# Loading the first x tile in two column pieces, one on each DMA queue, with 15 warm-up matmuls instead of 18

## The chip, the cores and the metric

The kernel runs on one core of a Trainium2 chip. The metric is the device time of one execution in microseconds (us). The profile's span, from the first to the last instruction, is about 1.8 us shorter than that time.

## The reference

A two-layer network with SiLU, forward and backward, all in bf16:

```python
# x [1, 2048, 640], w1 [640, 1536], w2 [1536, 640], grad_out like x
h = jnp.einsum("bsd,df->bsf", x, w1)
out = jnp.einsum("bsf,fd->bsd", silu(h), w2)
# returned: out, and the gradients of x, w1 and w2 for grad_out
```

## The kernel before

The change touches only the first microseconds. The core starts its loads before anything else, and TensorE runs matmuls on a constant tile ("warm-ups") until x arrives. Three tiles of 128 rows of x (x0, x1, x2) are transposed on TensorE; then the product h = x·w1 starts with row block 0 of w1, whose columns 0 to 511 and 512 to 1023 are loaded separately. SyncE (SP) and ScalarE (ACT) each feed one DMA queue (q1 and q10 of the page: 146960 and 288 packets in before).

```python
    NWARM = 18
    ...
        early = [nc.vector.memset(warm[:], 1.0)]
        ...
        for i in range(NWARM):
            early.append(nc.tensor.matmul(wp[:, 0:P], lhsT=warm[:], rhs=warm[:], start=True, stop=True))
    ...
        def load_x(eng, q):
            return eng.dma_start(out=x_nat[:, q, :], in_=x_v[:, q, :])
    ...
        early += [load_x(nc.sync, 0), load_x(nc.scalar, 1), load_x(nc.sync, 2)]
        early += [load_w1(0, slice(0, FC), nc.scalar), load_w1(0, slice(FC, FA))]
        early += [load_w1(k, slice(0, FA)) for k in range(1, 3)]
        ...                                   # row blocks 3 and 4, the rest of w1
        nc.sync.dma_start(out=w2_nat[:], in_=w2_v[:])
        goT_next = load_goT(0)
    ...
        def pe_x(xT):                         # 5 transposes for each of x0, x1, x2
            ...
        def h_first(xT, aT, ghT):
            pe_x(xT)
            ...
            for dt_ in range(DT):             # row blocks of w1
                for ft in range(NA):          # ft 0..3 read columns 0..511, ft 4..7 the others
                    mm(ft, dt_, slice(0, HC), dt_ == 0, False)      # 384 columns of xT (x0, x1, x2)
            ...                               # then the last 128 columns, then 512-column matmuls
```

Of the kernel before, what the change touches and what calls it, by code (L numbers as in the profile page):

```python
# [75 lines left out]
def kernel(  # L76
# [11 lines left out]
    nc = tc.nc  # L88
    P = 128
# [6 lines left out]
    S, D = x2.shape  # L96
# [6 lines left out]
    NFC = F // FC  # L103
    FB = FC // P
    LAG = 2
    NWARM = 18
    NQ = 3
    HC = NQ * P
    NA = 8
    FA = NA * P  # L110
# [15 lines left out]
    x_nat = natpool.tile([P, ST, D], dt_in, name="x_nat")  # L126
# [3 lines left out]
    x_v = x2.rearrange("(st p) d -> p st d", p=P)  # L130
# [17 lines left out]
    with ExitStack() as mctx:  # L148
# [9 lines left out]
        early = [nc.vector.memset(warm[:], 1.0)]  # L158
        warm_a = cpool.tile([P, 1], FP32, name="warm_a")
        wp = ps_h.tile([P, SC], FP32, name="wp", tag="hp")  # L160
        for i in range(NWARM):
            early.append(nc.tensor.matmul(wp[:, 0:P], lhsT=warm[:], rhs=warm[:], start=True, stop=True))
# [18 lines left out]

        xT_next = xpool.tile([P, DT, SC], dt_in, name="xT")

        def load_x(eng, q):
            return eng.dma_start(out=x_nat[:, q, :], in_=x_v[:, q, :])

        def load_w1(k, cols=slice(0, F), eng=nc.sync):
            return eng.dma_start(out=w1_nat[:, k, cols], in_=w1_v[:, k, cols])

        early += [load_x(nc.sync, 0), load_x(nc.scalar, 1), load_x(nc.sync, 2)]  # L190
        early += [load_w1(0, slice(0, FC), nc.scalar), load_w1(0, slice(FC, FA))]
        early += [load_w1(k, slice(0, FA)) for k in range(1, 3)]
        for k in range(3, DT):
            load_w1(k, slice(0, FA))
        nc.sync.dma_start_transpose(out=xT_next[:, :, HC:SC], in_=x2[HC:SC, :])
        nc.sync.dma_start(out=w1_nat[:, :, FA:F], in_=w1_v[:, :, FA:F])
# [34 lines left out]
        def silu_a(ft, hp, aT):  # L231
            nc.scalar.activation(aT[:, ft, :], hp[:], ACT.Silu)  # L232
# [16 lines left out]
        def h_first(xT, aT, ghT):  # L249
# [3 lines left out]
            def mm(ft, dt_, cols, start, stop):  # L253
                nc.tensor.matmul(  # L254
                    hs[ft][:, cols],
                    lhsT=w1_nat[:, dt_, ft * P:(ft + 1) * P],
                    rhs=xT[:, dt_, cols],
                    start=start,
                    stop=stop,
                )  # L260

            for dt_ in range(DT):
                for ft in range(NA):
                    mm(ft, dt_, slice(0, HC), dt_ == 0, False)
            for ft in range(NA):
                for dt_ in range(DT):
                    mm(ft, dt_, slice(HC, SC), False, dt_ == DT - 1)
                silu_a(ft, hs[ft], aT)
# [48 lines left out]
        for c in range(NCH):  # L317
# [10 lines left out]
            if c == 2:  # L328
                for j in range(0, ST, STC):
                    rows = slice(max(j, NQ), j + STC)  # L330
                    nc.sync.dma_start(out=x_nat[:, rows, :], in_=x_v[:, rows, :])

            if c == 0:
                h_first(xT, aT, ghT)
                nc.sync.dma_start(
                    out=aT_scr[:, c * SC:(c + 1) * SC].rearrange("(ft p) s -> p ft s", p=P), in_=aT[:]
                )
                sd_phase(c, w2_nat, aT, oT_scr)
                for ft in range(FT):
                    g_group(ft, goT, ghT)  # L340
                nc.sync.dma_start(
                    out=ghT_scr[:, c * SC:(c + 1) * SC].rearrange("(ft p) s -> p ft s", p=P), in_=ghT[:]
# [4 lines left out]
            for i in range(FT + LAG):  # L347
# [7 lines left out]
                out=aT_scr[:, c * SC:(c + 1) * SC].rearrange("(ft p) s -> p ft s", p=P), in_=aT[:]  # L355
            )
            nc.sync.dma_start(
                out=ghT_scr[:, c * SC:(c + 1) * SC].rearrange("(ft p) s -> p ft s", p=P), in_=ghT[:]
# [7 lines left out]
    with ExitStack() as fctx:  # L366
# [45 lines left out]
        for fc in range(NFC):  # L412
            gh_blk = gh_blks[fc]
            for dt_ in range(DT):
                if dt_ == DT // 2:
                    store_gw2(fc)
                if fc == NFC - 1 and dt_ == DT - 1:
                    last_stores = []
                    for k, (lo, hi) in enumerate(((0, FC - P), (FC - P, FC))):
# [12 lines left out]
                        else:  # L432
                            nc.vector.tensor_copy(out=g1[:, lo:hi], in_=gp[:, lo:hi])  # L433
                        store = nc.sync.dma_start(
                            out=gw1_v[:, dt_, fc * FC + lo:fc * FC + hi], in_=g1[:, lo:hi]
# [50 lines left out]
```

## Time and profile before

| | before |
|---|---|
| time, median of the first 3 runs | 319.7 us (319.48 to 320.14) |
| span of the profiled run | 318.5 us |
| TensorE (PE) busy | 315.5 us |
| first transpose, first h matmul | 2.85 us, 4.53 us |
| first 512-column matmul of h | 13.86 us |

The page of the profile first: busy time with its share of the span, then the chain that ended last.

```profile
span 318.5 us, 3634 instructions
...
PE 315.5 (99%) x1529; PEld 147.5 (46%) x1529; DVE 103.0 (32%) x183; ACT 77.4 (24%) x139; POOL 0.7 (0%) x6
...
PE 98%; DMA 1%; DVE 0%; issue 0%; DVEq 0%; SPq 0%
```

TensorE is the bottleneck nearly throughout, so work can be saved only at the start or the end. Now the start of the same chain in order of time. The columns are start, length (both us) and what the time was spent in.

```profile
...
0.08 2.73 DMA x_nat<-in_x_dram
2.81 0.05 issue
2.85 1.78 PE tp L212 x15
4.64 9.39 PE hp L254 x80
14.03 4.32 PE hp L223 x20
18.34 11.87 PE hp L302 x55
```

The chain starts with the load of x0, runs through the 15 transposes, and then stays on TensorE. Next is the timeline of the matmuls (PE) and their weight loads (PEld) of before: start, length, line, tiles, count, and in brackets the idle time before the group and what ended it. Here and below, "..." marks lines left out.

```profile
...
0.51 2.10 PE L162 MATMUL wp<-warm 128*128 128x128 bf16 x18 [0.51 <-DVE warm L158]
2.85 1.78 PE L212 MATMUL tp<-ident,x_nat 128*128 128x128 bf16 x15 [0.24 <-DMA x_nat<-in_x_dram]
...
4.33 0.31 PEld L254 LDWEIGHTS <-w_nat 128*128 128x128 bf16 x2
4.53 9.50 PE L254 MATMUL hp<-xT,w_nat 128*128 128x384 bf16 x80
...
4.80 0.15 PEld L254 LDWEIGHTS <-w_nat 128*128 128x128 bf16 x1 [0.17 <-issue]
...
5.12 0.15 PEld L254 LDWEIGHTS <-w_nat 128*128 128x128 bf16 x1 [0.17 <-issue]
5.45 0.72 PEld L254 LDWEIGHTS <-w_nat 128*128 128x128 bf16 x4 [0.17 <-issue]
...
6.42 7.44 PEld L254 LDWEIGHTS <-w_nat 128*128 128x128 bf16 x72 [0.25 <-DMA w_nat<-in_w_dram]
...
13.86 4.48 PE L223 MATMUL hp<-xT,w_nat 128*128 128x512 bf16 x20
```

The single weight loads at 4.80, 5.12 and 5.45 us are 0.32 us apart: this is a 384-column matmul at half clock. Later ones are 0.16 us apart and merge into one line. The trace's clock record says the same: full speed from 5.71 us. The PE clock row of the page is too coarse to show this. PE idled only 0.45 us before x0, and 0.10 us before the first h matmul. Idle times in this text are counted so: from start to start, less one matmul. The brackets count from a modelled end, and so show less (0.24).

### The profile page before, as it was taken

How to read it: one execution, taken by the hardware profiler on the slowest of the kernel's cores; microseconds unless marked ns; L12 is line 12 of the kernel's file. 1: busy time of each engine (PE TensorE's matmuls, PEld its weight loads, DVE VectorE, ACT ScalarE, POOL GpSimd, SP SyncE). 2: the span in 40 equal slices, each digit the busy share in tenths (PEclk: the TensorE clock that was granted, in tenths of full speed). 3: DMA queues.
4: the chain of work that ended last, by engine and by line, in shares of the span. 5: the costliest groups of instructions: out<-in, count | busy, mean ns of one | idle time of the engine just before them, and what ended most of it. 6: DMA issues, size and time to landing. Idle time of an engine off the chain costs nothing.

```text
span 318.5 us, 3634 instructions
## 1 busy us (share of the span) xinstructions
PE 315.5 (99%) x1529; PEld 147.5 (46%) x1529; DVE 103.0 (32%) x183; ACT 77.4 (24%) x139; POOL 0.7 (0%) x6
## 2 busy tenths in 40 slices
PE   9999999999999999999999999999999999999997
PEld 6644444444444444444444444444444444444444
DVE  1387641477410187710147741000000100001001
ACT  3492000644201354411064520110100001001010
POOL 0000000000000000000000000000000000000000
PEclk9999999999999999999999999999999999999999
DMA  9999999999799874492635079919999999996011
GB/s 242 332 182 190 238 283 239 350 291 311 233 229 320 199 228 113 145 302 83 166 105 145 0 259 268 216 24 299 254 243 261 251 209 341 245 264 217 33 35 49
DMA packets 147264, 66.85 MB, mean 210 GB/s; under 512 B 113328, under 2 KB 146736, under 8 KB 147248
## 3 DMA queue, kind: packets, MB, share of 16 engines
q1 hardware_dynamic: 146960, 66.33, 82.6%
q10 hardware_dynamic: 288, 0.30, 0.3%
q8 instruction: 12, 0.20, 0.2%
q14 instruction: 4, 0.03, 0.0%
HBM read 9.18 MB, written 28.97 MB: 120 GB/s over the span
## 4 chain that ended last, share of the span: by engine, by line
PE 98%; DMA 1%; DVE 0%; issue 0%; DVEq 0%; SPq 0%
PE hp L302 33%; PE hp L286 16%; PE hp L391 16%; PE hp L442 15%; PE hp L223 14%; PE hp L254 3%; PE hp L422 1%; DMA x_nat<-in_x_dram 1%; PE tp L212 1%; DVE g L433 0%; DVEq L433 0%; SPq L470 0%
## 5 line engine op out<-in xcount | busy, mean ns | idle before, releaser
L286 PE MATMUL hp<-goT,w2T 128*128 128x512 bf16 x240 | 56.9, 379 | 0.0
L302 PE MATMUL hp<-aT,w_nat 128*128 128x512 bf16 x240 | 52.5, 379 | 0.0
L302 PE MATMUL hp<-ghT,w1T 128*128 128x512 bf16 x240 | 52.5, 379 | 0.0
L391 PE MATMUL hp<-a_blk,go_nat 128*128 128x512 bf16 x240 | 52.0, 379 | 0.0
L442 PE MATMUL hp<-gh_blk,x_nat 128*128 128x512 bf16 x224 | 48.5, 379 | 0.0
L223 PE MATMUL hp<-xT,w_nat 128*128 128x512 bf16 x200 | 48.2, 379 | 0.0
L310 ACT ACTIVATE oT<-hp 128x512 bf16<-128x512 f32 x24 | 14.4, 598 | 104.3 <-PE hp L302 104.3
L232 ACT ACTIVATE aT<-hp 128x512 bf16<-128x512 f32 x48 | 28.5, 614 | 37.4 <-PE hp L223 30.4
L302 PEld LDWEIGHTS <-w1T 128*128 128x128 bf16 x240 | 23.5, 98 | 28.3
L302 PEld LDWEIGHTS <-w_nat 128*128 128x128 bf16 x240 | 23.5, 98 | 28.3 <-DMA w_nat<-in_w_dram 0.2
L391 PEld LDWEIGHTS <-go_nat 128*128 128x128 bf16 x240 | 23.5, 98 | 28.3
L286 PEld LDWEIGHTS <-w2T 128*128 128x128 bf16 x240 | 23.5, 98 | 28.3
L293 DVE SCALAR_TENSOR_TENSOR ghT<-ghT,hp 128x512 bf16<-128x512 bf16 x48 | 32.5, 682 | 7.0 <-PE hp L286 7.0
L442 PEld LDWEIGHTS <-x_nat 128*128 128x128 bf16 x224 | 21.9, 98 | 26.4
L312 DVE CAST oT<-hp 128x512 bf16<-128x512 f32 x16 | 11.0, 691 | 70.6 <-PE hp L302 70.6
L239 DVE SCALAR_TENSOR_TENSOR ghT<-aT,v 128x512 bf16<-128x512 bf16 x48 | 32.6, 686 | 0.3
L223 PEld LDWEIGHTS <-w_nat 128*128 128x128 bf16 x200 | 19.5, 98 | 23.4
L238 DVE TENSOR_SCALAR v<-t 128x512 bf16<-128x512 f32 x48 | 20.1, 425 | 28.1 <-ACT t L236 28.1
L236 ACT ACTIVATE t<-hp 128x512 f32<-128x512 f32 x44 | 26.5, 620 | 0.0
L453 DVE CAST g<-hp 128x512 bf16<-128x512 f32 x7 | 4.8, 692 | 47.0 <-PE hp L442 28.0
L401 DVE CAST g2T<-hp 128x512 bf16<-128x512 f32 x7 | 4.8, 692 | 46.1 <-PE hp L391 46.1
L399 ACT ACTIVATE g2T<-hp 128x512 bf16<-128x512 f32 x8 | 4.8, 597 | 47.0 <-PE hp L391 47.0
(24 smaller groups left out, 43.7 us busy)
## 6 DMA issues: line engine op xcount, KB each, us to landing
aT_scr<-aT SPq DMA_DIRECT2D x4, 1536.0 KB, 6.2
ghT_scr<-ghT SPq DMA_DIRECT2D x4, 1536.0 KB, 8.0
out_dram<-o_sb SPq DMA_DIRECT2D x8, 640.0 KB, 3.5
oT_scr<-oT SPq DMA_DIRECT2D x4, 640.0 KB, 4.3
go_nat<-in_grad_out_dram SPq DMA_DIRECT2D x4, 640.0 KB, 6.5
gxT_scr<-oT SPq DMA_DIRECT2D x4, 640.0 KB, 5.7
w_nat<-in_w_dram SPq DMA_DIRECT2D x1, 1920.0 KB, 12.5
x_nat<-in_x_dram SPq DMA_DIRECT2D x3, 640.0 KB, 7.0
```

The lines of the kernel that those rows point to most:

```text
L223: nc.tensor.matmul(hp[:], lhsT=w1_nat[:, dt_, ft * P:(ft + 1) * P], rhs=xT[:, dt_, :], start=(dt_ == 0), stop=(dt_ == DT - 1),)
L232: nc.scalar.activation(aT[:, ft, :], hp[:], ACT.Silu)
L236: nc.scalar.activation(t[:], hp[:], ACT.Tanh, scale=0.5)
L238: nc.vector.tensor_scalar(out=v[:], in0=t[:], scalar1=-0.5, scalar2=0.5, op0=ALU.mult, op1=ALU.add)
L239: nc.vector.scalar_tensor_tensor(out=ghT[:, ft, :], in0=aT[:, ft, :], scalar=1.0, in1=v[:], op0=ALU.subtract, op1=ALU.mult)
L286: nc.tensor.matmul(gp[:], lhsT=w2T[:, dt_, ft * P:(ft + 1) * P], rhs=goT[:, dt_, :], start=(dt_ == 0), stop=(dt_ == DT - 1),)
L293: nc.vector.scalar_tensor_tensor(out=ghT[:, ft, :], in0=ghT[:, ft, :], scalar=1.0, in1=gp[:], op0=ALU.add, op1=ALU.mult)
L302: nc.tensor.matmul(op_[:], lhsT=w_all[:, ft, dt_ * P:(dt_ + 1) * P], rhs=rhs_all[:, ft, :], start=(ft == 0), stop=(ft == FT - 1),)
L310: nc.scalar.activation(oT[:, dt_, :], op_[:], ACT.Copy)
L312: nc.vector.tensor_copy(out=oT[:, dt_, :], in_=op_[:])
L391: nc.tensor.matmul(gp[:], lhsT=go_nat[:, st, dt_ * P:(dt_ + 1) * P], rhs=a_blk[:, st, :], start=(st == 0), stop=(st == ST - 1),)
L442: nc.tensor.matmul(gp[:], lhsT=x_nat[:, st, dt_ * P:(dt_ + 1) * P], rhs=gh_blk[:, st, :], start=(st == 0), stop=(st == ST - 1),)
```

## The change

It aims to have x0 on chip sooner: 256 of its 640 columns on SyncE's queue and the other 384 on ScalarE's, ahead of x1 and x2. With x0 sooner, fewer warm-ups fill the wait.

```diff
-    NWARM = 18
+    NWARM = 15
     NQ = 3
+    HD = 2 * P
...
-        def load_x(eng, q):
-            return eng.dma_start(out=x_nat[:, q, :], in_=x_v[:, q, :])
+        def load_x(eng, q, cols=slice(0, D)):
+            return eng.dma_start(out=x_nat[:, q, cols], in_=x_v[:, q, cols])
...
-        early += [load_x(nc.sync, 0), load_x(nc.scalar, 1), load_x(nc.sync, 2)]
+        early += [load_x(nc.sync, 0, slice(0, HD)), load_x(nc.scalar, 0, slice(HD, D))]
+        early += [load_x(nc.sync, 1), load_x(nc.scalar, 2)]
         early += [load_w1(0, slice(0, FC), nc.scalar), load_w1(0, slice(FC, FA))]
```

## The prediction

> **What bounds the kernel now.** TensorE. On the page, PE is busy 315.5 us of a 318.5 us span, and the chain of waits is 98% PE and 1% "DMA x_nat<-in_x_dram": the start, until the first x tile is in. Only that start can change. In the chain in order of time: DMA of x until 2.81 us, 15 transposes of x from 2.85, the matmuls of h from then on without a gap.
>
> **The start, from the trace's single records.** Landings: x0 2.81, x1 3.23, x2 3.63, both pieces of w1 row block 0 by 4.33, w1 block 1 6.37, block 2 7.11 us. Warm-up matmuls come every 107 ns from 0.51 to about 2.40; PE then waits 0.45 us for x0. Transposes come every 107 ns and end near 4.43; x1 and x2 are in before PE needs them. The first h matmul starts at 4.53, after a VectorE copy. Matmuls of 384 columns are 320 ns apart until 5.71 and 163 ns after: the clock record turns to full speed there. PE asks for w1 block 1 at 6.39, which landed at 6.37: no slack. Block 2 has over 0.5 us.
>
> **The DMA side.** On each DMA engine x0, x1 and x2 follow each other: completion packets of x0 and of x1 (other queue) are 420 ns apart, x1 to x2 420 to 480. So x0 does not share its engines with x1; it is already served first. A 1280-byte packet takes 55 ns, 1024 takes 46, 2048 takes 84. By that line (estimate) 512 bytes take 27 and 768 take 37: 8 + 8 packets are 0.51 us, against 0.44 in one piece. What makes x0 late is the start: first packets from 1.12, some stalled for 0.5 to 0.7 us, which splitting does not remove. [...]
>
> **What the change does (estimates).**
> - Columns 0 to 255 of x0 land 0.2 us sooner (2.6), the rest at about 2.9, 0.07 later than all of x0 now. Two transposes start early, three wait.
> - x1 and x2 land 0.07 later (3.30, 3.70). PE then waits for x1: transposes end near 4.37, not 4.43. Gain 0.06 us.
> - w1 block 1 may be 0.07 later (6.44), which eats that gain. Net on the path -0.05 to +0.05 us.
> - ScalarE issues one more DMA (0.4 us), so its table load ends near 2.9; its first copy is at 4.14: free.
> - Three warm-ups fewer: they were off the path. [...]
>
> **Prediction.** 319.6 us, range 319.2 to 320.2. Faster by over 2%: 0.5%; within 2%: 99%; slower: 0.5%. The spread of before (0.66 us) exceeds the effect.
>
> **What would show it.** Right: first transpose near 2.6, a wait for x0's second piece and for x1, first h matmul at 4.4 to 4.55, w1 block 1 asked for at 6.3 to 6.45. Wrong: all of x0 in before 2.6, first h matmul before 4.3[...].

The marked cuts took out a rule on turns of the DMA queues, an allowance for a later full clock in some runs, and the sign that went with it: no trace of this case had shown them. The terms sum to -0.05 to +0.05 us on the path. The forecast was 319.6 us, beside the 319.7 us of before's first runs; the 0.1 us between them lies within their spread (0.66 us).

## The result, and the profile after

| | before | after |
|---|---|---|
| time, median of 6 runs each | 320.19 us (319.48 to 320.91) | 322.35 us (321.67 to 323.21) |
| ratio | | 1.0069 (1.0044 to 1.0093) |
| span of the profiled run | 318.5 us | 321.0 us |
| x0 wholly landed | 2.81 us | 2.33 us |
| x1 landed | 3.23 us | 3.71 us |
| first half of w1 block 0 landed | 4.01 us | 5.42 us |
| first h matmul | 4.53 us | 5.47 us |
| full clock from | 5.71 us | 9.92 us |
| first 512-column matmul of h | 13.86 us | 16.39 us |

The change is within 2%, but clearly slower: about 2.2 us. The page of after:

```profile
span 321.0 us, 3601 instructions
...
PE 315.4 (98%) x1498; PEld 147.6 (46%) x1526; DVE 103.0 (32%) x183; ACT 77.4 (24%) x139; POOL 0.7 (0%) x6
...
PE 98%; DMA 1%; issue 1%; DVE 0%; SPq 0%; DVEq 0%
```

Busy time is as before; the span is 2.5 us longer. (The trace lacks some matmul records: 1498, beside 1526 weight loads.) The start of the chain of after:

```profile
...
0.54 3.17 DMA x_nat<-in_x_dram
3.71 0.05 issue
3.75 1.26 PE tp L214 x10
5.02 0.02 issue
5.04 0.44 DVE xT L219
5.48 11.08 PE hp L256 x80
```

The chain no longer starts with x0. It starts with the load issued at 0.54 us, x1, and only 10 transposes are on it; the 80 matmuls of h take 11.08 us instead of 9.39. The timeline of after, same columns:

```profile
...
0.51 1.78 PE L163 MATMUL wp<-warm 128*128 128x128 bf16 x15 [0.51 <-DVE warm L159]
2.15 0.73 PE L214 MATMUL tp<-ident,x_nat 128*128 128x128 bf16 x5
...
3.75 1.25 PE L214 MATMUL tp<-ident,x_nat 128*128 128x128 bf16 x10 [0.88 <-DMA x_nat<-in_x_dram]
...
5.46 0.13 PEld L256 LDWEIGHTS <-w_nat 128*128 128x128 bf16 x2 [0.73 <-DMA w_nat<-in_w_dram]
5.47 11.09 PE L256 MATMUL hp<-xT,w_nat 128*128 128x384 bf16 x80 [0.47 <-DVE xT L219]
...
9.28 0.15 PEld L256 LDWEIGHTS <-w_nat 128*128 128x128 bf16 x1 [0.17 <-issue]
9.60 0.15 PEld L256 LDWEIGHTS <-w_nat 128*128 128x128 bf16 x1 [0.17 <-issue]
9.92 6.46 PEld L256 LDWEIGHTS <-w_nat 128*128 128x128 bf16 x65 [0.17 <-issue]
...
16.39 3.83 PE L225 MATMUL hp<-xT,w_nat 128*128 128x512 bf16 x16
```

There are two waits: for x1 (1.08 us between the fifth transpose and the sixth) and for the first half of w1 block 0 (0.67 us). The chain names a VectorE copy for the second one, since that copy ended at 5.47; but the weight load's own line names the DMA of w, which landed at 5.42. In before the first h matmul started 0.57 us ahead of the end of the same copy, so the copy is not what it needs. After that, weight loads stay 0.32 us apart until 9.92 us: 14 matmuls at half clock, against 4.

The two parts add up. The first h matmul is 0.94 us later, and 10 more matmuls cost 0.157 us more each (320 less 163 ns): 0.94 + 1.57 = 2.51 us. The 512-column matmuls start 2.53 us later, the span is 2.5 us longer, and nothing is lost after that.

### The profile page after: what moved, and what is told of

It is laid out like the page before. It is cut to its first block, busy times and chain, and to the rows that moved or that the text cites. A ratio compares the mean times of both kernels' runs of the same rounds, so it can differ in the third digit from the quotient of the medians.

```text
span 321.0 us, 3601 instructions
## 1 busy us (share of the span) xinstructions
PE 315.4 (98%) x1498; PEld 147.6 (46%) x1526; DVE 103.0 (32%) x183; ACT 77.4 (24%) x139; POOL 0.7 (0%) x6
## 4 chain that ended last, share of the span: by engine, by line
PE 98%; DMA 1%; issue 1%; DVE 0%; SPq 0%; DVEq 0%
PE hp L304 32%; PE hp L288 16%; PE hp L393 16%; PE hp L444 15%; PE hp L225 13%; PE hp L256 3%; PE hp L424 1%; DMA x_nat<-in_x_dram 1%; PE tp L214 0%; DVE xT L219 0%; SPq L186 0%; DVE g L435 0%; DVEq L435 0%; SPq L472 0%
```

## The experiments

The theories. **Clock theory**: TensorE idles too much in the early microseconds, so full clock comes later, and the slow matmuls are the loss. **Arrival theory**: data come later, PE waits for them, and the clock follows along or matters little. Both can hold in part; the runs were to split the 2.2 us. All runs gave correct results, each in 5 rounds against before on the same chip; ratios are to before. "Lands" and "full clock" are from the one profiled run of each kernel. The landing times of all of them stand in one table after the last experiment.

### k1_warm15: only fewer warm-ups

```diff
-    NWARM = 18
+    NWARM = 15
```

> Before with 15 warm-up matmuls, loads untouched. Clock theory (the time is lost because [...] full clock comes later): PE idles about 0.75 us before the first transpose instead of 0.45, so full clock comes somewhat later on average; +0.1 to +0.7 us, ratio 1.0005 to 1.002. Arrival theory (the time is lost because the split makes x1 and the first w1 pieces land late, and PE waits for them): loads as before, so 0, ratio 1.000 within 0.0007; the first h matmul near 4.53 us.

Measured: 320.34 us, ratio 1.0009 (0.9992 to 1.0026). No difference is shown; a cost of the size that the clock theory named is not excluded. The warm-ups alone are not the loss.

### k2_split18: only the split

The changed kernel with `NWARM = 18`.

> The split loads with 18 warm-up matmuls. Both theories: most of the loss is here. Clock theory: the gaps for x1 and for w1 block 0 remain, the gap before the first transpose is about nil; ratio 1.004 to 1.007, full clock after 7 us in the profile. Arrival theory: first h matmul near 5.4 us and ratio about 1.007, as with 15. If instead the number of warm-ups were the cause: ratio 1.000.

Measured: 322.27 us (319.67 to 323.11), ratio 1.0052 (1.0022 to 1.0083). The loads carry most of the loss. This kernel's profiled run was one of its quick ones (320.78 us): w1 block 0 was as late as in after (5.56 us), but the clock was already full when the first h matmul came at 5.61, and the 512-column matmuls started at 14.36 us. So the expected "full clock after 7 us" failed in this profile. It shows late data without a late clock: 0.5 us behind before, not 2.5.

### k3_split15_fill: the changed kernel with 16 unread matmuls, so that PE has no gaps

```diff
+    FILL = (10, 0, 6)
...
+        def fill(n):
+            for _ in range(n):
+                nc.tensor.matmul(wp[:, 0:P], lhsT=warm[:], rhs=warm[:], start=True, stop=True)
...
+                    fill(FILL[q])             # in the source after the transposes of tile q; on the chip before all of them
```

> The changed kernel plus 16 matmuls on the constant tile that nobody reads: 10 after the transposes of x0 and 6 after those of x2, where PE idled 1.1 and 0.7 us. They bring no data earlier. Clock theory: full clock comes by 7 us; the time falls by 1.2 to 2 us against the changed kernel, ratio to before 1.001 to 1.003. Arrival theory: no gain, ratio 1.007 or more.

Measured: 320.9 us, ratio 1.0024 (1.0008 to 1.0039). The chain of this kernel's start:

```profile
...
0.51 1.78 PE wp L164 x15
2.29 1.71 PE wp L210 x16
3.99 1.60 PE tp L219 x15
5.59 9.28 PE hp L262 x80
```

The edit did not do what the expectation says. All sixteen unread matmuls (line 210) ran straight after the warm-ups, before the first transpose, which began at 3.79 us instead of 2.15. So they did not fill the gaps. They held the transposes back until x1 was in (3.37 us), and no gap opened: after 0.51 us PE idled only 0.10 us. The first h matmul came at 5.48 us, as in after (5.47), here because the transposes were late, for w1 was in at 4.49. In this profile the loads came sooner than in after, as they vary from run to run, but that gained nothing, since the first h matmul was no earlier. Yet about two thirds of the loss went (ratio 1.0024 instead of 1.0069), with full clock at 6.52 us instead of 9.92. This is the clock theory's run, and it holds.

### k4_warm8: the gap alone, loads untouched

```diff
-    NWARM = 18
+    NWARM = 8
```

> Before with 8 warm-up matmuls: PE idles from 1.36 us to the landing of x0 near 2.8; loads untouched. Clock theory: [...] +0.6 to +1.6 us, ratio 1.002 to 1.005, and more spread. Arrival theory: the warm-ups are off the data path, ratio 1.000 within 0.0007.

Measured: 321.03 us, ratio 1.0029 (1.001 to 1.0047). In the profile the data were even early, and the first h matmul came at 4.26 us; the clock was full at 6.76 only. PE idle time costs 0.9 us here with no change in any load. The arrival theory can't give this.

### k5_split15_fill5: a smaller filling

As k3 with `FILL = (5, 0, 0)`. These five too ran before the first transpose, like five more warm-ups.

> The changed kernel with only 5 unread matmuls after the transposes of x0 and none before the first h matmul: about 0.5 us of PE idle taken away where x1 is waited for, and no delay added. Clock theory [...]: better than the changed kernel by 1 us or more, ratio to before 1.000 to 1.003; full clock by 7 us in most runs. Arrival theory (late x1 and w1 block 0 alone): as the changed kernel, 1.006 to 1.007.

Measured: 320.69 us (319.89 to 322.66), ratio 1.0031 (1.0004 to 1.0058). Four runs had spans of 318.1 to 319.2 us and two had 320.9. Full clock may have come later in those two, since the last gap stayed open; that is a guess, and no profile of them shows it. In the profile full clock came at 3.44 us, w1 block 0 at 5.74.

### k6_warm22: before with more warm-ups

`NWARM = 22` in before.

> Before with 22 warm-up matmuls instead of 18, so that PE idles hardly at all before x0 lands at 2.6 to 2.8 us. Clock theory: [...] ratio 0.9985 to 1.000; first h matmul at most 0.1 us later. Arrival theory: 1.000.

Measured: 320.52 us, ratio 1.0009 (0.9997 to 1.0021). The clock theory's gain did not come. Full clock came at 5.48 us, 0.23 us sooner than in before, but PE then waited 0.40 us for w1 block 1 (in at 6.62). In this profile that wait ate the quicker start. There was no wait for w2, which landed at 18.18 us; its product started at 18.43.

### k7_split15_x2sp: w1 block 0 back to second place on ScalarE's queue

```diff
-        early += [load_x(nc.sync, 1), load_x(nc.scalar, 2)]
+        early += [load_x(nc.sync, 1), load_x(nc.sync, 2)]
```

> The changed kernel with x2 on the SyncE queue, so that the ScalarE queue carries the second piece of x0 and then the first piece of w1 block 0, as the second of its queue as in before. If the late landing of w1 block 0 (5.4 and 5.6 us in two of three profiles of the split) comes from its place as third on ScalarE's queue, that piece lands by 4.5 us and the ratio falls to 1.002 or less. If it comes from slow packets of w1 whatever the place, the ratio stays at 1.004 to 1.007.

Measured: 321.67 us, ratio 1.0046 (1.0031 to 1.0062). The first half of w1 landed at 3.77 us, as expected of its place in the queue. The ratio did not fall as expected: PE still idled 0.78 us for x1, full clock came at 8.49 us, and most of what followed on SyncE's queue came later (w1 block 2, say, at 8.70 us instead of 7.29). Half right.

### k8_whole_swap: the exchange of x1 and x2 without a split

```diff
-        early += [load_x(nc.sync, 0), load_x(nc.scalar, 1), load_x(nc.sync, 2)]
+        early += [load_x(nc.sync, 0), load_x(nc.sync, 1), load_x(nc.scalar, 2)]
```

> Before (18 warm-up matmuls, x0 whole on SyncE), but with x1 on SyncE and x2 on ScalarE, as the change has them. If the exchange of queues is the cost: ratio 1.003 or more. If the split of x0 is: ratio 1.000 within 0.0015, x0 in by 2.8 us, w1 block 0 by 4.5 us.

Measured: 320.8 us, ratio 1.0023 (1.0011 to 1.0035), spans all 319.0 to 319.5. x1 landed at 3.61 us instead of 3.23: the second place on SyncE's queue costs it that with x0 whole too. Full clock came early (4.67 us), and the 512-column matmuls started at 13.52 us, ahead of before. The lead was lost afterwards. The waits of PE in its first 20 us, in total, times, longest:

```profile
PE hp L302 <- DMA w_nat<-in_w_dram: 0.6, 1, 0.6
PE wp L162 <- DVE warm L158: 0.5, 1, 0.5
PE tp L212 <- DMA x_nat<-in_x_dram: 0.4, 1, 0.4
```

The first line is new: PE waits for w2, which landed at 18.58 us here and at 18.04 in before. A quicker start can run into this floor.

### k9_before_w2halves and k10_swap_w2halves: w2 in two halves

```diff
-        nc.sync.dma_start(out=w2_nat[:], in_=w2_v[:])
+        for lo in range(0, FT, FT // 2):
+            nc.sync.dma_start(out=w2_nat[:, lo:lo + FT // 2, :], in_=w2_v[:, lo:lo + FT // 2, :])
```

> Before with w2 loaded in two halves of its 12 row blocks, first half first. In the profiles of before the product with w2 started at 18.18 us and w2 had landed at 18.04: a floor just under the start. If that floor counts: runs whose full clock comes early gain up to 0.5 us, ratio 0.9980 to 0.9995. If it does not: 1.000 within 0.0007.

Measured: 319.55 us (319.38 to 319.87) against 320.31, ratio 0.9977 (0.9965 to 0.9989). This beats both kernels, by 0.7 us. In its profile the first half of w2 landed at 13.26 us, the second at 17.36, and PE went on at 17.76 without a wait. The gain is measured; that the floor is all of it is only argued, since in this one profile even the second half was in time.

> The kernel with x1 and x2 exchanged between the queues (x0 whole, 18 warm-ups; ratio 1.0023) with w2 in halves. In its profile PE was ahead of before (512-column matmuls from 13.52 us, before 13.86) and then waited 0.6 us for w2, in at 18.58. If that wait was its whole loss: ratio 0.9985 to 1.0005, and no wait for w2 in the profile. If not: 1.002 stays.

Measured: 320.64 us (319.66 to 322.35), ratio 1.0019 (0.9996 to 1.0042). The wait for w2 is gone from the profile (PE went on at 18.25 us, the second half was in at 16.08), but the mean did not move clearly from the 1.0023 of k8, and spans now spread from 317.9 to 320.6 us. Inconclusive on how much of k8's loss the floor was.

### k11_rowhalves: x0 split by rows instead of columns

```diff
-        early += [load_x(nc.sync, 0, slice(0, HD)), load_x(nc.scalar, 0, slice(HD, D))]
+        early += [
+            eng.dma_start(out=x_nat[h:h + 64, 0, :], in_=x_v[h:h + 64, 0, :])
+            for eng, h in ((nc.sync, 0), (nc.scalar, 64))
+        ]
```

> The changed kernel (15 warm-ups, three loads on ScalarE's queue), but x0 split by partitions: 64 rows of 1280 bytes on each queue, as many descriptors as before. If the short reads of 512 and 768 bytes make the first w1 pieces late: they land by 4.6 us and the ratio is 1.001 to 1.003. If the place as third on ScalarE's queue or the earlier order does: they land after 5 us and the ratio is 1.005 to 1.007.

Measured: 323.07 us, ratio 1.0083 (1.0053 to 1.0113); the first half of w1 landed at 5.85 us, full clock came at 8.60. The loss stays without short reads. (Here the second load of each queue was also issued later, at 0.72 us and 0.79 instead of 0.54 and 0.62.)

### k12_split15_w1one: w1 block 0 as one load

```diff
-        early += [load_w1(0, slice(0, FC), nc.scalar), load_w1(0, slice(FC, FA))]
+        early += [load_w1(0, slice(0, FA))]
```

> The changed kernel, but w1 block 0 as one load of 1024 columns on SyncE instead of two of 512 on two queues: as many loads and descriptors before the matmuls as before, two loads on ScalarE's queue. If the extra load (descriptors, third on the queue) makes w1 block 0 late: it lands by 4.6 us, ratio 1.001 to 1.004. If the short reads of x0 do: after 5 us, ratio 1.005 to 1.008.

Measured: 321.54 us, ratio 1.0045 (1.0031 to 1.0058); w1 block 0 landed at 5.14 us, 15 of its 16 shares by 4.67. Between the two expectations; inconclusive on its own.

### k13_whole_w1third: no split, w1 block 0 in third place

```diff
-        early += [load_x(nc.sync, 0), load_x(nc.scalar, 1), load_x(nc.sync, 2)]
+        early += [load_x(nc.sync, 0), load_x(nc.scalar, 1), load_x(nc.scalar, 2)]
```

> Before (x0 whole, 18 warm-ups), x2 moved to ScalarE's queue, so that the first half of w1 block 0 is third there; SyncE has one load less in front. If the place in the queue is the cause: that half lands after 4.5 us, first h matmul with it, ratio 1.002 to 1.005. If the short reads of the split are: it lands by 4.3 us, ratio within 0.0015 of 1.000.

Measured: 323.39 us, ratio 1.0114 (1.0092 to 1.0135), the slowest of all. The chain of its start:

```profile
...
0.62 0.45 ACTq L185
1.07 0.03 issue
1.10 5.25 DMA w_nat<-in_w_dram
6.35 0.05 issue
6.40 10.59 PE hp L254 x80
```

The third load on ScalarE's queue took 5.25 us from issue to landing and everything waited for it, with x0 in one piece. It is more than expected: x2 was late too (4.91 us). Here the clock record even shows full clock granted at 3.96 us, taken back at 7.37 and granted again at 10.79. PE had idled 1.46 us for x2 and 1.16 us for w1 before it was taken back.

### k14_split15_w1swap: the split, halves of w1 block 0 exchanged

```diff
-        early += [load_w1(0, slice(0, FC), nc.scalar), load_w1(0, slice(FC, FA))]
+        early += [load_w1(0, slice(0, FC)), load_w1(0, slice(FC, FA), nc.scalar)]
```

> The changed kernel with the halves of w1 block 0 exchanged: the first half (columns 0 to 511, read by the first four h matmuls) third on SyncE, the second third on ScalarE. If the place in the queue is the cause: first half by 4.5 us, first h matmul at 4.5 to 4.9, the second PE gap gone, ratio 1.001 to 1.004 against 1.0069 of the change. If it is the split as such: first half after 5 us, ratio 1.006 or more.

Measured: 321.78 us, ratio 1.0059 (1.0035 to 1.0083). The first half landed at 5.09 us, x1 at 3.99. My expectation failed: in this kernel the third place on SyncE's queue was no better than the third on ScalarE's.

### k15_split18_repaired: the split with everything mended that could be

The exchange of k14, `NWARM = 18`, `FILL = (3, 0, 0)`, and w2 in halves. The three unread matmuls ran before the first transpose, so PE in effect had 21 warm-ups.

> The split with 18 warm-ups, 3 unread matmuls after the transposes of x0, the halves of w1 block 0 exchanged and w2 in two halves. If the split is worth something once repaired: ratio below 0.9977, that of before with w2 in halves alone. If x1 and w1 bind whatever x0 does: 0.9975 to 1.001.

Measured: 320.62 us (320.46 to 320.69), ratio 1.0013 (1.0 to 1.0026). The clock was full at 4.80 us and x1 in at 3.10, but w1 block 0 landed at 5.27 and the first h matmul came at 5.31. Without the split, w2 in halves gave 0.9977. The ratio lies above both expectations: the split has no gain to show even here.

### All profiles side by side

Times in us, one profiled run of each kernel. "w1 first half" is columns 0 to 511 of block 0, with its place: A2 is second on ScalarE's queue, A3 third there, S3 third on SyncE's.

| kernel | x0 | x1 | w1 first half | first h matmul | full clock | 512-column matmuls |
|---|---|---|---|---|---|---|
| before | 2.81 | 3.23 | 4.01 (A2) | 4.53 | 5.71 | 13.86 |
| after | 2.33 | 3.71 | 5.42 (A3) | 5.47 | 9.92 | 16.39 |
| k1 | 2.67 | 3.03 | 4.27 (A2) | 4.64 | 6.87 | 14.45 |
| k2 | 2.38 | 3.06 | 5.56 (A3) | 5.61 | by 5.61 | 14.36 |
| k3 | 2.39 | 3.37 | 4.49 (A3) | 5.48 | 6.52 | 14.71 |
| k4 | 2.55 | 2.95 | 3.85 (A2) | 4.26 | 6.76 | 14.21 |
| k5 | 2.39 | 3.50 | 5.74 (A3) | 5.79 | 3.44 | 14.53 |
| k6 | 2.64 | 3.05 | 3.91 (A2) | 4.52 | 5.48 | 14.11 |
| k7 | 2.50 | 3.57 | 3.77 (A2) | 4.75 | 8.49 | 15.28 |
| k8 | 2.47 | 3.61 | 3.94 (A2) | 4.79 | 4.67 | 13.52 |
| k9 | 2.69 | 3.06 | 3.96 (A2) | 4.40 | 5.07 | 13.45 |
| k10 | 2.58 | 3.68 | 4.11 (A2) | 4.87 | 5.58 | 13.93 |
| k11 | 2.79 | 3.38 | 5.85 (A3) | 5.90 | 8.60 | 15.96 |
| k12 | 2.44 | 3.91 | 5.14 (S3) | 5.19 | 6.99 | 14.81 |
| k13 | 2.40 | 2.83 | 6.35 (A3) | 6.40 | 3.96, lost 7.37 to 10.79 | 16.82 |
| k14 | 2.24 | 3.99 | 5.09 (S3) | 5.17 | 7.90 | 15.23 |
| k15 | 2.41 | 3.10 | 5.27 (S3) | 5.31 | 4.80 | 14.06 |

Three things can be read from it.

1. In second place on ScalarE's queue, the first half of w1 landed at 3.77 to 4.27 us in all eight profiles, with the split (k7) and without. In third place on either queue it landed at 4.49 to 6.35 in all nine others, with the split and without (k13). A third place is not late in itself, though: the second half of block 0 was third on SyncE's queue in before, and in at 4.33 (more under "What stays open").
2. x1 as first on ScalarE's queue landed at 2.83 to 3.23 us (before, k1, k4, k6, k9, k13); as second on SyncE's at 3.06 to 3.99.
3. The end of the start follows from two columns alone. From k5 and k2, where all matmuls ran at full clock, the 512-column matmuls come 8.74 us after the first h matmul. Each us spent at half clock after the first h matmul adds 0.5 us. For after: 5.47 + 8.74 + 0.5 × (9.92 − 5.47) = 16.4. Only k6, with its further wait of 0.40 us for w1 block 1, is over 0.1 us off.

## Why the prediction was wrong

I said 319.6 us, 319.2 to 320.2; measured 322.35. Point by point:

- **"What makes x0 late is the start ... which splitting does not remove": wrong.** I predicted 2.6 and 2.9 us for the two pieces; they landed at 2.10 and 2.33. The slow first packets of x0, up to 0.68 us in before, were not there in after; slow ones came a tile later, among x1's (up to 0.59 us). In the other seven kernels with column pieces, three to six packets of x0 took more than 0.15 us, at most 0.43. Over all profiles x0 landed at 2.24 to 2.50 us in column pieces and at 2.40 to 2.81 whole, so the 0.48 us between before and after is more than the usual gain.
- **"x1 and x2 land 0.07 later (3.30, 3.70)": wrong in size.** 3.71 and 3.88. I counted the extra packet time of short reads and not the place in the queue.
- **"w1 block 1 may be 0.07 later ... Net on the path -0.05 to +0.05 us": this is one step that failed.** The item that bound was one I had not costed: the first half of w1 block 0, moved from second to third on ScalarE's queue. It landed 1.41 us later, and the first h matmul came 0.94 us later, 5.47 instead of the 4.4 to 4.55 predicted. k13 shows the same lateness with no split at all, and k7 the early landing with it.
- **"Three warm-ups fewer: they were off the path": the other failed step.** A later full clock was allowed for in some runs only, as a tail risk and from the wrong gap. The warm-ups alone cost nothing clear (k1). It was the waits for x1 and w1 that opened the gaps, 1.08 and 0.67 us, and full clock came at 9.92 us instead of 5.71. In the profiled runs that cost 1.57 us. k3 and k4 show it from both sides: with the split but only 0.10 us of gaps, full clock came at 6.52 us; with fewer warm-ups and the loads untouched, only at 6.76.
- **The signs that it had named for "wrong"**: all of x0 before 2.6 us came (2.33), and the first h matmul before 4.3 us did not (5.47).
- **Right:** the table load on ScalarE ended at 2.96 us and was off the path; there was no effect near 2%.

The prediction's idea that x1 binds once x0 is early ("PE then waits for x1") was right, and that is also why the change could not gain: x0 was never alone at the head of the path. What it pushed back was needed just as soon.

How the 2.2 us of the mean splits: in k3, where PE had no gaps, 0.24% or 0.8 us stays, and in its profile the first h matmul is as late as in after; the other 1.4 us went with the gaps. The profiles of before and after split much the same way: 0.94 us of lateness and 1.57 us at half clock. Both theories held, the clock theory for the larger part.

**Idle time before full clock.** In k13's clock record the changes at 3.96, 7.37 and 10.79 us are 3.41 and 3.42 us apart, and the 314.03 us of full clock in before are 92 times 3.413 us. So I laid out the profiles in stretches of 3.41 us; that the clock goes by such stretches in every run is not shown. Full clock came at 3.44 to 9.92 us in the profiles, and nothing recorded tells where the stretches of another run would begin. Counting PE's idle time in the stretch that ended where full clock began, and in the one before it:

| | idle in the stretch of 3.41 us |
|---|---|
| stretches that ended in full clock: before, k1, k3, k4, k5, k6, k8 to k15 | 0.09 to 0.91 us |
| stretches that did not: after, k1, k4, k7, k11, k12, k14 | 1.10 to 1.83 us |
| one that did not: k3 (its first 0.81 us lie before PE's first matmul) | 0.81 us |

(after, k7: stretches laid out from the change of spacing, for the clock record is missing there; k2 left out, since its clock turned while PE idled. The time before PE's first matmul at 0.51 us is counted as idle: it is all of k3's 0.81 and 0.47 of k1's 1.10, for instance.) By this count before has only 0.55 us of gaps after 0.51 us, less than any refused stretch had; after has 1.75 us in two gaps near each other, more than any accepted one. That most runs of after would so reach full clock only once the second gap is over is my estimate from one profile of each kernel; the other runs have no record of it.

**What stays open.** Why a third place costs a whole microsecond and more. By an estimate from packet times it should cost a few tenths: one load of 128 KB took each DMA engine some 0.37 us (8 packets of 46 ns). In most of the late profiles the DMA engines were also less busy between 2.75 and 4 us (share of time with a packet under way, by quarters of a us: 0.80 to 0.89 in after, 0.90 to 1.02 in before), and single packets of w1 block 0 took up to 0.51 us in after.

The trace also has when each of the 16 DMA engines finished its share of a load, which says where the time goes. A load is in when its last share is (in after the last of w1's first half landed at 5.42 us, and the weight load that waited for it began at 5.46). The shares of the first half of w1 block 0 landed from 3.21 us on in before, eight of them by 3.50 and the last at 4.01; in after from 3.89 on, eight by 4.20 and the last at 5.42. So 0.7 us of the 1.41 hold for the middle of the shares: the second half of block 0, which came after it in before, now came ahead of it (eight shares by 4.00 us in before, by 3.94 in after). The other 0.7 us are a few late shares. Other loads have them in other profiles: in before w1 block 1 had eight shares by 4.76 us and the last at 6.37, and in k7 the second half of block 0 had 15 shares by 4.51 us and the last at 5.47. That second half, third on SyncE's queue, landed at 4.08 to 5.17 us in the seven kernels with x0 whole other than k13. What makes a share late no run here tells.

## What to carry to other kernels

Before moving a load to the front, write down every load that it moves back and when each is needed: here, in the profiles, x0 came 0.48 us sooner, and two items needed soon after it came 0.48 and 1.41 us later. Look at gaps of the matmul engine in the first microseconds not only for their own length, but for the full clock that they can delay: here, in the profiles, 1.75 us of gaps cost another 1.6 us at half clock, and unread matmuls that left PE no gap largely gave that back. Check in the trace that such an insertion ran where the source has it: in k3 it did not. And when a start has been tuned, look for the next floor before polishing it more: here it was a load needed at 18 us, and cutting that load in two was worth more (0.23%) than any of the starts tried here.

## What else the profiles show

- Stretches of 3.41 us, laid out as above, with up to 0.91 us of idle ended in full clock and seven with 1.10 us or more did not; one with 0.81 us did not either, so idle time alone does not draw the line. In k13 a stretch with 2.15 us of idle at full clock ended in half clock; in k5 one with 1.78 us did not.
- In that count transposes against the identity are not idle time. In before the stretch that ended in full clock held 0.55 us of idle and 1.6 us of transposes; with them as idle time it would have had 2.15 us (k10's 2.51), more than the refused one of k1 (1.10 and 0.74 us of transposes, 1.84), so the count would no longer part the two.
- Some packets of these first loads were slow. Of x0's in before, the slowest took 0.68 us where the usual one took 0.055; in after x0's took at most 0.08, and x1's up to 0.59. They are not only at the start: of w1's 2048-byte ones in before, the slowest took 0.79 us where the usual one took 0.084.
- A place in the queue, for these small loads side by side: second place meant 3.77 to 4.27 us and third 4.49 to 6.35 for the first half of w1 block 0, and third place 4.08 to 5.17 us for the second half in the kernels with x0 whole (k13 aside, where it was second).
